# Load queues, builder engine and emission order changed in a fused state-space and local-attention kernel

## The chip, the cores and the metric

The kernel runs on one core of a Trainium2 chip. The metric is the device time of one execution in microseconds (us). A kernel's time is the median of several executions. The profile that is read here is one execution, recorded by the hardware profiler; its span runs from the first to the last instruction and is about 2 us shorter than the time (231.0 us of 232.73 for the kernel before).

The engines are named as in the profile: PE is the matrix engine (TensorE), PEld its weight loads, DVE is VectorE, ACT is ScalarE, POOL is GpSimd, SP is SyncE. A "q" behind a name (ACTq, SPq) means an instruction that issues a DMA transfer from that engine's queue.

## The reference, cut to what matters

Two independent parts share one output. Part A is a diagonal complex state-space layer over 2048 steps of width 448. Part B is attention of 16 heads, each query looking at 8 keys at distances 0, 2, ..., 14.

```python
# part A
dt = exp(log_dt);  Lam_bar = exp(dt * Lam)
B_bar = ((Lam_bar - 1.0) / Lam)[:, None] * Bmat
h_t = Lam_bar * h_{t-1} + B_bar @ x_t                  # 2048 steps
y = 2 * Re(C @ h) + x * Dskip
# part B
q, k, v = split(x @ wqkv);  W, dil = 8, 2
attn = softmax(q . k[pos - 2*w] * scale, masked at the start)
out_B = (attn @ v) @ wo
# concatenate(y, out_B)
```

Part A needs the powers of `Lam_bar` (1, 2, 3, 4, 8, ... 1024 and some negative ones). They come from four small parameter vectors (Lambda_re, Lambda_im, log_dt, Dskip, together under 4 KB) by a long chain of small VectorE operations, the "setup".

## The kernel before

The kernel cuts the recurrence into blocks, so that most of it becomes matmuls. Each complex power becomes a block matrix "identity pattern times coefficient": the ten power matrices `Mm`, four matrices `MB` for B, three matrices `MC` for C. Part B works in five groups: `proj` (projection to q, k, v), four `unit`s (scores, exponential, mask, values, normalisation), `wo` (output projection). The program uses a framework with a scheduler: the order of calls sets priorities, and the scheduler then orders each engine's instructions. Each engine works off its own list in order; several waits below come from that (one of 21.1 us on ScalarE).

The parts that the change touches (cuts marked `...`):

```python
    def loads_params(self):
        self.pr = pool.tile([NPR, P], bf16, name="pr")
        for i, src in enumerate((self.A_Lre, self.A_Lim, self.A_logdt, self.A_Dskip)):
            nc.scalar.dma_start(self.pr[NM * i:NM * (i + 1), 0:PL], src.rearrange("(m p) -> m p", p=PL))

    def loads_b(self):                     # B, 2 x 392 KB
        nc.gpsimd.dma_start(self.bX[0:PL], ...)
        nc.gpsimd.dma_start(self.bX[PL:P], ...)
    # loads_c: cn, 8 x 98 KB on nc.gpsimd;  loads2: wo_p, 4 x 98 KB on nc.gpsimd
    # load_x, loads_x: transposing loads of x on nc.sync;  wqkv: nc.scalar

    def setup(self):
        V.tensor_copy(self.pr[:, PL:P], self.pr[:, 0:PL])      # needs all four parameter loads
        nc.tensor.transpose(pp[:], self.pr[:], ident[0:NPR, 0:NPR])
        ...                                                    # some 60 small VectorE operations
        self.ScB = coeffs("ScB", sa, sb, 4)
        self.ScM = coeffs("ScM", pw_re[:, 3:13], pw_im[:, 3:13], NMAT)

    def build(self, eng, out, Sc, i):      # two inputs, both in SBUF
        eng.tensor_tensor(out, self.Dm[:]...to_broadcast([P, NM, 2, PL]),
                          Sc[:, i]...to_broadcast([P, NM, 2, PL]), op=ALU.mult)

    # main program
    b.loads()                              # x block, wqk
    ...
    a.loads_params()
    b.loads_v()
    b.prep()                               # VectorE permutes wqk into wqk_p
    b.load_x(0, 1)
    a.loads_b()
    ...                                    # first projection with a.setup() in it
    b.load_x(1, 0); b.load_x(1, 1)
    a.b_mats(V)
    a.loads_x()
    for hg in range(4):
        b.unit(0, hg)
    a.loads_c()
    for m in range(NM):
        a.b_variant(m)                     # bv_ps = bX x MB, evicted to Bv
    b.loads2()
    a.setup_dg()
    b.proj(1)
    a.mats(G)                              # ten power matrices on GpSimd
    for hg in range(4):
        b.unit(1, hg)
    b.wo(0)
    for hg in range(4):
        a.l1(hg)                           # l_ps: 112 matmuls with Bv
    b.proj(2)
    ...
    a.l2()                                 # e_ps: first use of the power matrices
```

The softmax here doesn't subtract the row's maximum and nothing guards it: scores larger than these inputs give would overflow.

Of the kernel before, what the change touches and what calls it, by code (L numbers as in the profile page):

```python
# [12 lines left out]
bf16 = mybir.dt.bfloat16  # L13
# [3 lines left out]
P = 128  # L17
KT = 4
H = 16
DH = 28  # L20
NM = 7
PL = 64
# [12 lines left out]
NMAT = len(MATS)  # L35
# [12 lines left out]
class PartB:  # L48
# [38 lines left out]
    def loads2(self):  # L87
        nc, pool = self.nc, self.pool
        self.wo_p = pool.tile([P, 4, D], bf16, name="wo_p")
        nc.gpsimd.memset(self.wo_p[:], 0.0)  # L90
        wo_v = self.B_wo.rearrange("(g h d) c -> h d g c", g=4, d=DH)
        for h in range(4):
            nc.gpsimd.dma_start(self.wo_p[32 * h:32 * h + DH, :, :], wo_v[h])

    def prep(self):
        nc, pool, V, G = self.nc, self.pool, self.nc.vector, self.nc.gpsimd
# [104 lines left out]
class PartA:  # L201
# [8 lines left out]
    def loads_params(self):  # L210
        nc, pool = self.nc, self.pool
        self.pr = pool.tile([NPR, P], bf16, name="pr")
        for i, src in enumerate((self.A_Lre, self.A_Lim, self.A_logdt, self.A_Dskip)):
            nc.scalar.dma_start(self.pr[NM * i:NM * (i + 1), 0:PL], src.rearrange("(m p) -> m p", p=PL))

    def loads_b(self):
        nc, pool = self.nc, self.pool
        self.bX = pool.tile([P, NM, D], bf16, name="bX", tag="r0")
        nc.gpsimd.dma_start(self.bX[0:PL], self.A_Bre.rearrange("(m p) d -> p m d", p=PL))
        nc.gpsimd.dma_start(self.bX[PL:P], self.A_Bim.rearrange("(m p) d -> p m d", p=PL))  # L220

    def loads_x(self):
        nc, pool = self.nc, self.pool
# [6 lines left out]
    def loads_c(self):  # L230
        nc, pool = self.nc, self.pool
        self.cn = pool.tile([112, 4, NM, 2, PL], bf16, name="cn", tag="c7")
        for ri, src in enumerate((self.A_Cre, self.A_Cim)):
            for a in range(4):
                nc.gpsimd.dma_start(self.cn[:, a, :, ri, :],
                                    src[112 * a:112 * (a + 1)].rearrange("p (m q) -> p m q", q=PL))

    def c_transpose(self):
# [10 lines left out]
    def setup(self):  # L249
        nc, pool, V, G = self.nc, self.pool, self.nc.vector, self.nc.gpsimd  # L250
# [51 lines left out]
        pw_re, pw_im = sh, ch  # L302
# [31 lines left out]
        V.tensor_tensor(self.Dm[:], ident[:, 0:PL], ident[:, PL:P], op=ALU.add)  # L334

        def coeffs(name, re, im, n, conj=False):
            Sc = pool.tile([P, n, NM, 2], bf16, name=name, tag=("ScM" if name == "ScM" else "ScB"))
            s0, s1 = (1.0, -1.0) if conj else (-1.0, 1.0)
            V.tensor_copy(Sc[0:PL, :, :, 0], re[0:PL])
            V.tensor_copy(Sc[PL:P, :, :, 1], re[PL:P])  # L340
            V.tensor_scalar(Sc[PL:P, :, :, 0], im[PL:P], s0, None, op0=ALU.mult)
            V.tensor_scalar(Sc[0:PL, :, :, 1], im[0:PL], s1, None, op0=ALU.mult)
            return Sc

        self.ScB = coeffs("ScB", sa, sb, 4)
        self.ScM = coeffs("ScM", pw_re[:, 3:13], pw_im[:, 3:13], NMAT)
        self.mkC = lambda: coeffs("ScC", pw_re[:, 0:3], pw_im[:, 0:3], 3, conj=True)
        self.dsk = dsk

# [15 lines left out]
                V.tensor_scalar(self.Dg[h, k, :], self.ident[h], self.dsk[h, m:m + 1], None, op0=ALU.mult)  # L365

    def mats(self, eng):
        self.M = self.pool.tile([P, NMAT, NM, 2, PL], bf16, name="Mm")
        for i in range(NMAT):
            self.build(eng, self.M[:, i], self.ScM, i)  # L370
# [131 lines left out]
@with_exitstack  # L502
def kernel(
    ctx: ExitStack,
    tc: tile.TileContext,
    A_x: bass.AP,
    A_Lambda_re: bass.AP,
    A_Lambda_im: bass.AP,
    A_B_re: bass.AP,
    A_B_im: bass.AP,  # L510
    A_C_re: bass.AP,
    A_C_im: bass.AP,
    A_log_dt: bass.AP,
    A_Dskip: bass.AP,
    B_x: bass.AP,
    B_wqkv: bass.AP,
    B_wo: bass.AP,
    out: bass.AP,
):
    nc = tc.nc  # L520
    pool = ctx.enter_context(tc.tile_pool(name="sb", bufs=1))
    psum = ctx.enter_context(tc.tile_pool(name="ps", bufs=1, space=bass.MemoryType.PSUM))
    ident = pool.tile([P, P], bf16, name="ident")
    nc.vector.memset(ident[:], 0.0)
    warm = pool.tile([1, 1], f32, name="warm")
    nc.vector.memset(warm[:], 0.0)
    nc.scalar.activation(warm[:], warm[:], ACT.Exp)

    class _Ps:
        def tile(self, shape, dtype, name, tag):  # L530
            return psum.tile(shape, dtype, name=name, tag=tag, bufs={"s": 2, "o": 1, "mm": 3}[tag])
    ps = _Ps()

    b = PartB(tc, B_x, B_wqkv, B_wo, out, pool, ps)
    a = PartA(tc, A_x, A_Lambda_re, A_Lambda_im, A_B_re, A_B_im, A_C_re, A_C_im, A_log_dt, A_Dskip,
              out, ident, pool, ps)
    V, G = nc.vector, nc.gpsimd
    b.loads()
    nc.gpsimd.affine_select(out=ident[:], in_=ident[:], compare_op=ALU.not_equal, fill=1.0, base=0,
                            pattern=[[-1, P]], channel_multiplier=1)  # L540
    b.mask = pool.tile([P, P], bf16, name="mask")
    nc.vector.memset(b.mask[:], 1.0)
    nc.gpsimd.affine_select(out=b.mask[:], in_=b.mask[:], compare_op=ALU.is_ge, fill=0.0, base=-1,
                            pattern=[[-1, P]], channel_multiplier=1)
    nc.gpsimd.affine_select(out=b.mask[:], in_=b.mask[:], compare_op=ALU.is_ge, fill=0.0, base=HALO,
                            pattern=[[1, P]], channel_multiplier=-1)
    a.loads_params()
    b.loads_v()
    b.prep()
    b.load_x(0, 1)  # L550
    a.loads_b()
    steps = b.proj_steps(0)
    for _ in range(PRE):
        next(steps)
    a.setup()
    for _ in steps:
        pass
    b.load_x(1, 0)
    b.load_x(1, 1)
    a.b_mats(V)  # L560
    a.loads_x()
    for hg in range(4):
        b.unit(0, hg)
    a.loads_c()
    for m in range(NM):
        a.b_variant(m)
    b.loads2()
    a.setup_dg()
    b.proj(1)
    a.mats(G)  # L570
    for hg in range(4):
        b.unit(1, hg)
    b.wo(0)
    for hg in range(4):
        a.l1(hg)
    b.proj(2)
    a.c_mats(V)
    a.c_transpose()
    for hg in range(4):
        b.unit(2, hg)  # L580
    b.wo(1)
    b.proj(3)
    a.l2()
    a.c_variants()
    for hg in range(4):
        b.unit(3, hg)
    b.wo(2)
    a.hfull(0)
    a.hfull(1)
    b.proj(4)  # L590
    b.unit(4, 0)
    a.hfull(2)
    a.hfull(3)
    b.unit(4, 1)
    a.hfull(4)
    a.hfull(5)
    b.wo(3)
    a.hfull(6)
    for s in range(4):
        if s >= 2:  # L600
            b.unit(4, s)
        for i in range(4):
            a.y(i, s)
    b.wo(4)
# [29 lines left out]
```

## Time and profile before

| | before |
|---|---|
| time, median of the runs beside the changed kernel's | 231.98 us (229.49 to 232.91) |
| span of the profiled run | 231.0 us |
| PE busy | 171.3 us, 74% |
| VectorE busy | 140.2 us, 61% |
| GpSimd busy | 35.3 us, 15% |

The page of the profile draws the span in 40 equal slices of 5.8 us. Each digit is the busy share of a slice in tenths; PEclk is the granted clock of PE in tenths of full speed; the DMA row is the mean busy share of the 16 DMA engines.

```profile
PE   0241197013445999999999999999989199999994
...
DVE  4200199999999793697441019909889964814261
...
PEclk9999999755575599999999999998579959999999
DMA  6999999600000000020000001100000200222212
```

PE is nearly idle in the first five slices (0 to 29 us), while the DMA engines are at work. VectorE is full from slice 5 to 12 (counted from 0), and PE is at most half busy from slice 7 to 12. Only from slice 13 (75 us) is PE mostly full. A change for the front part of the kernel can therefore win much, one for the back part little.

The timeline of the queue of ScalarE (start, duration, engine, line, instruction, times; in brackets idle time before it and what ended it) shows how the start is held up:

```profile
1.90 0.82 ACTq L214 DMA_DIRECT2D pr<-in_A_Lambda_re_dram  x1
...
4.93 0.30 ACTq L214 DMA_DIRECT2D pr<-in_A_Lambda_im_dram  x1
14.50 0.28 ACTq L214 DMA_DIRECT2D pr<-in_A_log_dt_dram  x1
22.43 0.27 ACTq L214 DMA_DIRECT2D pr<-in_A_Dskip_dram  x1
...
23.90 1.48 ACT L134 CAST qT<-qk_ps 128x480 bf16<-128x480 f32 x3 [21.14 <-DMA pr<-in_A_Dskip_dram]
```

The four tiny parameter loads are issued at 1.9, 4.9, 14.5 and 22.4 us. The compiled instruction list tells why: each but the first waits until an earlier load has landed:

```
before, ScalarE
5 L214 DMACopy pr<-in_A_Lambda_re_dram 7x64
6 L214 DMACopy pr<-in_A_Lambda_im_dram 7x64 [waits DMAHW0_49]
7 L214 DMACopy pr<-in_A_log_dt_dram 7x64 [waits DMAHW2_49]
8 L214 DMACopy pr<-in_A_Dskip_dram 7x64 [waits DMAHW4_49]
9 L76 DMACopy wv<-in_B_wqkv_dram 128x3x448 [waits DMAHW5_49]
```

In the program, DMAHW0 is the counter of the first load of weights, DMAHW2 that of the second load for the first x block, DMAHW4 that of the second load for the second x block. In the trace these three land at 4.91, 14.48 and 22.41 us, each 0.02 us before the issue that waits for it. So two of the four tiny loads wait for loads of x on SyncE's queue.

Behind these issues in ScalarE's list stand the first evictions of q, which come at 23.9 us after 21.1 us of idle time. On VectorE the copy that starts the setup waits for the last parameter:

```profile
7.02 1.47 DVE L98 COPY wqk_p<-wqk_nat 128x1792 bf16<-128x1792 bf16 x2 [3.15 <-DMA wqk_nat<-in_B_wqkv_dram]
27.90 0.17 DVE L256 COPY pr<-pr 28x64 bf16<-28x64 bf16 x1 [19.40 <-DMA pr<-in_A_Dskip_dram]
```

Then the second piece of trouble. GpSimd builds the ten power matrices from 37.9 us, as its timeline shows:

```profile
37.94 17.54 POOL L351 TENSOR_TENSOR Mm<-Dm,ScM 128x896 bf16<-128x896 bf16 x10 [16.77 <-DVE ScM L340]
```

These are VectorE's setup operations of the same time, and the four B matrices, from its timeline:

```profile
37.89 0.17 DVE L316 TENSOR_TENSOR sa<-lm_187,prT 128x7 f32<-128x7 f32 x1
38.09 1.56 DVE L318 TENSOR_TENSOR sa<-sa,t_190 128x7 f32<-128x7 f32 x1
39.68 1.61 DVE L319 TENSOR_TENSOR sa<-sa,rden 128x7 f32<-128x7 f32 x1
41.21 0.15 DVE L321 TENSOR_TENSOR t_190<-lm_187,prT 128x7 f32<-128x7 f32 x1
41.32 1.63 DVE L326 TENSOR_TENSOR sa<-kf,sa 128x21 f32<-128x21 f32 x1
...
53.97 2.37 DVE L341 TENSOR_SCALAR ScB<-sb 64x28 bf16<-64x28 f32 x1
...
57.01 4.08 DVE L351 TENSOR_TENSOR MB<-Dm,ScB 128x896 bf16<-128x896 bf16 x4
```

An operation on 7, 21 or 28 columns takes 0.15 to 0.18 us when it is not held up. The slow ones take 1.5 us and more, while a build lasts 1.79 us on average. The B matrices MB are complete at 61.1 us, and only then do the B variants (bv_ps), the second projection and the first layer (l_ps) follow. From 103.9 us on the first layer runs without a break:

```profile
103.88 19.72 PE L429 MATMUL l_ps<-xa,Bv 128*128 128x512 bf16 x88
```

### The profile page before, as it was taken

The page shows a single profiled execution, that of the slowest core. Times are in us where ns is not written, and L with a number is a line of the kernel's source. Part 1 is how long each engine was busy: PE and PEld are TensorE (multiplying, and loading weights), DVE is VectorE, ACT ScalarE, POOL GpSimd, SP SyncE. Part 2 cuts the span into 40 slices and gives each one's busy share as a digit, 9 for nine tenths or more (in the row PEclk, how much of TensorE's full clock was granted, in tenths as well). Part 3 has the DMA queues.
Part 4 walks back from the last instruction along what each step waited for, and adds up shares of the span by engine and source line. Part 5 has one row for each costly group of instructions (what it writes and reads, how often), then busy time and mean ns, then how long its engine had stood idle before and what let it go on. Part 6 is the DMA issues. An engine that isn't in the chain of part 4 may idle for free.

```text
span 231.0 us, 3482 instructions
## 1 busy us (share of the span) xinstructions
PE 171.3 (74%) x1348; PEld 86.9 (38%) x1348; DVE 140.2 (61%) x284; ACT 101.2 (44%) x177; POOL 35.3 (15%) x62
## 2 busy tenths in 40 slices
PE   0241197013445999999999999999989199999994
PEld 0010033002121244544444455465425096565652
DVE  4200199999999793697441019909889964814261
ACT  2000238113233566963335689665269148521311
POOL 8854004997000000000000000000000000000000
PEclk9999999755575599999999999998579959999999
DMA  6999999600000000020000001100000200222212
GB/s 195 155 157 161 207 213 189 147 0 3 0 0 0 1 3 0 19 59 0 0 3 0 0 1 38 38 0 0 3 0 19 60 0 3 70 79 76 67 61 70
DMA packets 26625, 12.11 MB, mean 52 GB/s; under 512 B 21056, under 2 KB 26048, under 8 KB 26608
## 3 DMA queue, kind: packets, MB, share of 16 engines
q1 hardware_dynamic: 24792, 8.67, 18.7%
q0 software_dynamic: 800, 2.01, 5.1%
q10 hardware_dynamic: 1016, 1.21, 1.7%
q8 instruction: 10, 0.16, 0.3%
q14 instruction: 7, 0.06, 0.1%
HBM read 3.21 MB, written 3.67 MB: 30 GB/s over the span
## 4 chain that ended last, share of the span: by engine, by line
PE 55%; DVE 25%; DMA 9%; ACT 5%; SPq 2%; issue 2%; ACTq 0%; DVEq 0%
PE l_ps L429 11%; PE qk_ps L129 11%; PE y_ps L488 9%; DMA xb_66<-in_B_x_dram 7%; PE v_ps L141 5%; PE bv_ps L394 4%; PE wo_ps L194 4%; DVE pt L169 4%; ACT pt L167 3%; PE cv_ps L411 2%; PE o_ps L175 2%; DMA pr<-in_A_Dskip_dram 2%; PE s_ps L160 2%; DVE tO L181 2%; DVE MB L351 2%
## 5 line engine op out<-in xcount | busy, mean ns | idle before, releaser
L167 ACT ACTIVATE pt<-s_ps 128x960 bf16<-128x960 f32 (+2 forms) x40 | 32.3, 878 | 21.1 <-PE s_ps L160 19.9
L169 DVE TENSOR_TENSOR pt<-pt,mask 128x960 bf16<-128x960 bf16 (+2 forms) x40 | 22.4, 560 | 29.8 <-ACT pt L167 29.6
L129 PE MATMUL qk_ps<-xb_66,wqk_p 128*128 128x480 bf16 (+5 forms) x96 | 22.7, 398 | 13.3 <-DMA xb_66<-in_B_x_dram 13.2
L129 PEld LDWEIGHTS <-wqk_p 128*128 128x128 bf16 x192 | 18.8, 118 | 29.4 <-issue 12.0
L429 PE MATMUL l_ps<-xa,Bv 128*128 128x512 bf16 x112 | 25.9, 379 | 0.0
L175 PE MATMUL o_ps<-pt,va 128*32 128x120 bf16 (+2 forms) x288 | 12.7, 230 | 17.6 <-DVE pt L169 14.5
L134 ACT CAST qT<-qk_ps 128x480 bf16<-128x480 f32 (+2 forms) x20 | 9.9, 507 | 27.5 <-DMA pr<-in_A_Dskip_dram 21.1
L351 POOL TENSOR_TENSOR Mm<-Dm,ScM 128x896 bf16<-128x896 bf16 x10 | 17.5, 1788 | 16.8 <-DVE ScM L340 16.8
L394 PE MATMUL bv_ps<-MB,bX 128*128 128x512 bf16 x28 | 13.1, 564 | 8.3 <-ACT Bv L399 3.8
L175 PEld LDWEIGHTS <-va 128*32 128x32 bf16 x288 | 7.1, 99 | 31.2 <-issue 28.1
L129 PE MATMUL qk_ps<-xb_67,wqk_p 128*128 128x480 bf16 (+5 forms) x96 | 18.6, 335 | 0.0
L194 PE MATMUL wo_ps<-wo_p,oT 128*120 128x448 bf16 (+2 forms) x72 | 17.5, 363 | 0.1
L160 PE MATMUL s_ps<-qT,kT 28*128 28x120 bf16 (+2 forms) x288 | 14.0, 226 | 3.3 <-ACT pt L167 3.1
L137 POOL MEMSET va<- 128x256 bf16 x5 | 1.6, 323 | 90.9 <-PE o_ps L175 90.9
L429 PEld LDWEIGHTS <-Bv 128*128 128x128 bf16 x112 | 10.6, 97 | 13.2 <-issue 1.4
L399 ACT CAST Bv<-bv_ps 128x512 bf16<-128x512 f32 x14 | 8.2, 586 | 15.8 <-PE bv_ps L394 15.6
L134 ACT CAST kT<-qk_ps 128x488 bf16<-128x488 f32 (+2 forms) x20 | 10.4, 518 | 7.1 <-PE qk_ps L129 7.0
L197 ACT CAST yb<-wo_ps 120x448 bf16<-120x448 f32 (+2 forms) x18 | 9.7, 579 | 8.3 <-PE wo_ps L194 8.3
L181 DVE STREAM_TRANSPOSE tO<-o_ps 128x480 f32<-128x480 f32 (+2 forms) x20 | 11.9, 597 | 1.6 <-PE o_ps L175 1.5
L256 DVE COPY pr<-pr 28x64 bf16<-28x64 bf16 x1 | 0.2, 169 | 19.4 <-DMA pr<-in_A_Dskip_dram 19.4
L186 DVE STREAM_TRANSPOSE oT<-on 128x480 bf16<-128x480 bf16 (+2 forms) x20 | 11.7, 586 | 0.2
L185 DVE TENSOR_TENSOR on<-tO,r 128x480 bf16<-128x480 f32 (+2 forms) x20 | 11.5, 576 | 0.2
(162 smaller groups left out, 270.7 us busy)
## 6 DMA issues: line engine op xcount, KB each, us to landing
out_dram<-ya SPq DMA_DIRECT2D x16, 112.0 KB, 1.7
out_dram<-yb SPq DMA_DIRECT2D x8, 105.0 KB, 1.9
out_dram<-yb SPq DMA_DIRECT2D x8, 98.0 KB, 1.8
wqk_nat<-in_B_wqkv_dram ACTq DMA_DIRECT2D x1, 672.0 KB
bX<-in_A_B_re_dram POOLq DMA_DIRECT2D x1, 392.0 KB, 10.1
bX<-in_A_B_im_dram POOLq DMA_DIRECT2D x1, 392.0 KB, 11.2
cn<-in_A_C_re_dram POOLq DMA_DIRECT2D x4, 98.0 KB, 12.4
cn<-in_A_C_im_dram POOLq DMA_DIRECT2D x4, 98.0 KB, 9.8
```

The source lines that it names most:

```text
L129: nc.tensor.matmul(ps[:, off:off + cnt], lhsT=self.wp[:, w, k, 4 * hg:4 * hg + 4].rearrange("p h d -> p (h d)"), rhs=self.xb[p][:, k, XP + ...
L134: nc.scalar.copy(dst[:, hg, 0:tot], ps[:, 0:tot])
L160: nc.tensor.matmul(sp[h // 2][:, h % 2, nq * i:nq * (i + 1)], lhsT=kT[32 * h:32 * h + DH, hg, koff[i]:koff[i] + P], rhs=qT[32 * h:32 * h + ...
L167: nc.scalar.activation(pt[:, :, 0:tot], sp[u][:, :, 0:tot], ACT.Exp, scale=scale)
L169: V.tensor_tensor(pv, pv, self.mask[:, 0:nq].unsqueeze(1).unsqueeze(1).to_broadcast([P, 2, nb, nq]), op=ALU.mult)
L175: nc.tensor.matmul(po[32 * h:32 * h + 32, nq * i:nq * (i + 1)], lhsT=va[:, i, 4 * hg + h, :], rhs=pts[h // 2][:, h % 2, nq * i:nq * (i + 1 ...
L181: V.transpose(tO[:, 0:nj].rearrange("p j d -> p (j d)"), po[:, 0:tot])
L194: nc.tensor.matmul(ps[0:nq, :], lhsT=oT[:, hg, nq * i:nq * (i + 1)], rhs=self.wo_p[:, hg, :], start=(hg == 0), stop=(hg == 3))
L351: eng.tensor_tensor(out, self.Dm[:].unsqueeze(1).unsqueeze(1).to_broadcast([P, NM, 2, PL]), Sc[:, i].unsqueeze(3).to_broadcast([P, NM, 2, ...
L394: nc.tensor.matmul(ps[:].rearrange("p s c -> p (s c)"), lhsT=self.bX[:, m, c0:c0 + P], rhs=self.MB[:, m].rearrange("p s h q -> p (s h q)") ...
L429: nc.tensor.matmul(ps[u][:], lhsT=self.Bv[:, s, KT * m + k, :], rhs=self.xT[:, k, s, :], start=(s == 0 and k == 0), stop=(k == KT - 1), sk ...
L488: nc.tensor.matmul(ps[:], lhsT=self.hl[m][:, s, i, :], rhs=self.Dv[s][:, m, :], start=(m == 0), stop=False, skip_group_check=True)
```

## The change

The intent: load what is needed first first, let VectorE instead of GpSimd build the power matrices, late enough not to delay anything, and give PE the second projection to do while VectorE works off setup and unit 0. There are four parts, called *parameters*, *bulk loads*, *matrices* and *order* below.

```diff
# parameters: first in the program, on GpSimd's queue
-            nc.scalar.dma_start(self.pr[NM * i:NM * (i + 1), 0:PL], ...)
+            nc.gpsimd.dma_start(self.pr[NM * i:NM * (i + 1), 0:PL], ...)
+    a.loads_params()
     b.loads()
 ...
-    a.loads_params()
     b.loads_v()
# bulk loads: bX, cn and wo_p from GpSimd's queue to SyncE's, bX ahead of the second x block
-        nc.gpsimd.dma_start(self.bX[...] / self.cn[...] / self.wo_p[...]
+        nc.sync.dma_start(self.bX[...] / self.cn[...] / self.wo_p[...]
     b.prep()
+    a.loads_b()
     b.load_x(0, 1)
-    a.loads_b()
# matrices: coefficients made on demand, matrices on VectorE behind the first layer
-            Sc = pool.tile([P, n, NM, 2], bf16, name=name, tag=("ScM" if name == "ScM" else "ScB"))
+            Sc = pool.tile([P, n, NM, 2], bf16, name=name, tag="ScB")
-        self.ScM = coeffs("ScM", pw_re[:, 3:13], pw_im[:, 3:13], NMAT)
+        self.mkM = lambda: coeffs("ScM", pw_re[:, 3:13], pw_im[:, 3:13], NMAT)
     def mats(self, eng):
+        self.ScM = self.mkM()
 ...
-    a.mats(G)
     for hg in range(4):
         b.unit(1, hg)
     b.wo(0)
     for hg in range(4):
         a.l1(hg)
+    a.mats(V)
     b.proj(2)
# order: second projection ahead of the B variants
     a.loads_c()
+    b.proj(1)
     for m in range(NM):
         a.b_variant(m)
     b.loads2()
     a.setup_dg()
-    b.proj(1)
```

More of the change, by code (lines that the diff above doesn't have):

```diff
@@ L92, in loads2 @@
         for h in range(4):
-            nc.gpsimd.dma_start(self.wo_p[32 * h:32 * h + DH, :, :], wo_v[h])
+            nc.sync.dma_start(self.wo_p[32 * h:32 * h + DH, :, :], wo_v[h])
     def prep(self):
@@ L213, in loads_params @@
         for i, src in enumerate((self.A_Lre, self.A_Lim, self.A_logdt, self.A_Dskip)):
-            nc.scalar.dma_start(self.pr[NM * i:NM * (i + 1), 0:PL], src.rearrange("(m p) -> m p", p=PL))
+            nc.gpsimd.dma_start(self.pr[NM * i:NM * (i + 1), 0:PL], src.rearrange("(m p) -> m p", p=PL))
     def loads_b(self):
@@ L218, in loads_b @@
         self.bX = pool.tile([P, NM, D], bf16, name="bX", tag="r0")
-        nc.gpsimd.dma_start(self.bX[0:PL], self.A_Bre.rearrange("(m p) d -> p m d", p=PL))
-        nc.gpsimd.dma_start(self.bX[PL:P], self.A_Bim.rearrange("(m p) d -> p m d", p=PL))
+        nc.sync.dma_start(self.bX[0:PL], self.A_Bre.rearrange("(m p) d -> p m d", p=PL))
+        nc.sync.dma_start(self.bX[PL:P], self.A_Bim.rearrange("(m p) d -> p m d", p=PL))
     def loads_x(self):
@@ L234, in loads_c @@
             for a in range(4):
-                nc.gpsimd.dma_start(self.cn[:, a, :, ri, :],
+                nc.sync.dma_start(self.cn[:, a, :, ri, :],
                                     src[112 * a:112 * (a + 1)].rearrange("p (m q) -> p m q", q=PL))
```

## The prediction

> **What bounds it now.** The span is 231.0 us and PE is busy 171.3 (74%). By stages: From 0 to 28 us PE has about 5 us of work: loads fill the DMA engines (0.6 to 1.27 of their time, 150 to 230 GB/s). From 28 to 100 us VectorE is the limit. From 100 us to the end PE is nearly full. The first-layer matmuls (l_ps) run without a break from 103.9 us; what is to win lies before.
>
> **Three waits there.**
> 1. Parameters. ScalarE issues the four small loads and each waits for an earlier transfer: issued at 1.9, 4.9, 14.5, 22.4 us. VectorE's setup starts only at 27.9 (19.4 us idle, released by the Dskip load), and ScalarE's first eviction of q waits 21.1 us behind the same issues.
> 2. GpSimd builds the power matrices from 37.9 to 55.4 us (10 x 1.79 us). Meanwhile eleven tiny VectorE operations take 1.53 to 1.66 us each, against 0.15 to 0.28 before: about 15 us. The Trainium skill ("SBUF — State Buffer", shared port pair) says a VectorE instruction with two SBUF inputs contends with a GpSimd one that reads SBUF and one fully blocks; the durations here, near GpSimd's 1.79, agree.
> 3. Unit 0, the B variants and the second projection run one after another (61 to 92 us).
>
> **What the change does.** Parameters go first on GpSimd and should land by 4 to 8 us. The bulk loads leave GpSimd; B follows the first x block on SyncE, so that block no longer shares with 2 MB of B, C and wo. I put its landing at 10 us instead of 14.5. ScalarE's queue is free for evictions after about 3 us. Twelve projection matmuls (0.42 us each) still precede the parameter transpose, so setup starts at about 15 us. Setup without slowed operations and without the ScM copies: about 11 us, MB 4 x 1.08: B matrices ready near 30 us instead of 61.  Then VectorE has unit 0 (12.4 us, the pace of later units), 14 Bv evictions (9.5), unit 1 (11.5): 33 us, perhaps 36 with waits, during which PE does projection 2 (9.4) and the variants. l_ps runs without a break at about 66 instead of 103.9: 38 us gained.
>
> **Given back.** Ten power matrices at 1.08 us plus ScM copies land on VectorE among the l_ps evictions; one step of l_ps lasts 1.8 us, an eviction 0.69 plus two matrices 2.85, so PE loses about 1 us in four or five steps: 4 us. The 127 us after are unchanged.
>
> **Prediction.** 232.7 - 38 + 4 = about 199 us; 191 to 209 should hold it 8 times in 10. Faster by over 2%: 0.96; within 2%: 0.03; slower: 0.01.
>
> **What the profile would show.** Right: first q eviction near 12 us, not 23.9; parameter copy before 9 us; setup operations all under 0.3 us; MB done near 30; uninterrupted l_ps near 66; small PE gaps in l_ps before VectorE evictions. Wrong: PE waiting for the second x block, B or wo on the single SyncE queue, whose issues wait for earlier transfers.
>
> **What would make me wrong.** The first x block landing as late as before: 4 to 5 us lost. Half granted clock, as from 42 to 83 us before: up to 5 us. In-order waits between VectorE, ScalarE and PE in the interleaved stage: up to 8 us. VectorE overloaded in l_ps: up to 6 us.

## The result

| | before | changed |
|---|---|---|
| time, median | 231.98 us (4 runs) | 192.94 us (192.16 to 193.89, 4 runs) |
| ratio of fast runs | | 0.8333, 95% interval 0.8248 to 0.8418 |
| span of the profiled run | 231.0 us | 191.9 us |
| PE busy | 171.3 us, 74% | 164.6 us, 86% |
| VectorE busy | 140.2 us, 61% | 133.5 us, 70% |
| GpSimd busy | 35.3 us, 15% | 8.9 us, 5% |
| mean granted PE clock | 0.889 | 0.956 |

A ratio is the mean time of one kernel's fast runs over that of the other's fast runs of the same rounds, so it is not quite the ratio of the medians. "Fast" is the state of the run; runs more than 1.5% above the fastest of the same kernel count as slow and are left out.

The time lies in the predicted range (191 to 209), 6 us under the predicted 199. The rows of PE, VectorE and the granted clock from the page of the changed kernel, with slices of 4.8 us now:

```profile
PE   0079994998999999999999999988945999999993
...
DVE  5027999799999999995029944988999278035161
...
PEclk9999998899999999999999999958995799999999
```

The idle front of PE is down to two slices, and PE is mostly full from there on. VectorE is just as full in the front part, but now PE works at the same time. The lines that answer to those of before, from the changed kernel's timeline of ScalarE:

```profile
12.48 0.56 ACT L134 CAST qT<-qk_ps 128x480 bf16<-128x480 f32 x1 [9.73 <-PE qk_ps L129]
```

From its timeline of VectorE:

```profile
9.80 0.17 DVE L256 COPY pr<-pr 28x64 bf16<-28x64 bf16 x1 [6.00 <-DMA pr<-in_A_Dskip_dram]
...
9.97 1.16 DVE L98 COPY wqk_p<-wqk_nat 128x1792 bf16<-128x1792 bf16 x2
...
24.64 0.18 DVE L326 TENSOR_TENSOR sa<-kf,sa 128x21 f32<-128x21 f32 x1
...
26.69 4.10 DVE L351 TENSOR_TENSOR MB<-Dm,ScB 128x896 bf16<-128x896 bf16 x4
```

And from its timeline of PE, the first layer from the point where it has PE to itself:

```profile
64.64 2.12 PE L430 MATMUL l_ps<-xa,Bv 128*128 128x512 bf16 x9
67.11 7.15 PE L430 MATMUL l_ps<-xa,Bv 128*128 128x512 bf16 x32 [0.35 <-DVE hl_899 L436]
74.71 8.00 PE L430 MATMUL l_ps<-xa,Bv 128*128 128x512 bf16 x36 [0.46 <-ACT hl_942 L434]
```

The first eviction of q comes at 12.48 us, the setup operations take 0.17 to 0.18 us, MB is complete at 30.8 us. Unit 1's last value matmuls start at 64.3 us, and from 64.6 us the first layer has PE to itself, as it had from 103.9 us before. The new brackets in the last two lines are small gaps of PE that the kernel before did not have.

One line was not foreseen. The parameter copy stands ahead of the permutation `wqk_p` in VectorE's list and waits until 9.80 us, because the parameters need 5.3 to 6.7 us from issue to landing. The first matmul therefore waits for `wqk_p`, not for the x block:

```profile
10.66 4.56 PE L129 MATMUL qk_ps<-xb_71,wqk_p 128*128 128x480 bf16 x12 [10.66 <-DVE wqk_p L98]
```

| landmark, us | before | predicted | changed |
|---|---|---|---|
| first q eviction | 23.9 | 12 | 12.5 |
| parameter copy | 27.9 | under 9 | 9.8 |
| setup starts (parameters transposed) | 28.4 | 15 | 15.4 |
| B matrices complete | 61.1 | 30 | 30.8 |
| first layer alone on PE | 103.9 | 66 | 64.6 |
| first power-matrix matmul (e_ps) | 154.2 | | 116.1 |
| end of span | 231.0 | | 191.9 |

So 39.2 us are gained by the time the first layer has PE to itself, 38.1 us are left at e_ps, and 39.1 us at the end. The gain is made in the front, as predicted. What the landmarks do not tell is which of the four parts made it.

### The profile page after: what moved, and what is told of

Its sections match the earlier page's. It is cut to its first block, busy times and chain, and to the rows that moved or that the text cites. A ratio compares the mean times of both kernels' runs of the same rounds, so it can differ in the third digit from the quotient of the medians.

```text
span 191.9 us, 3468 instructions
## 1 busy us (share of the span) xinstructions
PE 164.6 (86%) x1348; PEld 84.3 (44%) x1348; DVE 133.5 (70%) x294; ACT 99.8 (52%) x177; POOL 8.9 (5%) x42
## 4 chain that ended last, share of the span: by engine, by line
PE 66%; DVE 16%; ACT 9%; DMA 3%; issue 3%; POOL 1%; ACTq 0%; DVEq 0%; POOLq 0%
PE qk_ps L129 14%; PE l_ps L430 13%; PE y_ps L489 11%; PE v_ps L141 6%; PE wo_ps L194 5%; ACT pt L167 5%; PE o_ps L175 4%; DMA pr<-in_A_Dskip_dram 3%; PE s_ps L160 3%; PE cv_ps L412 3%; DVE pt L169 2%; PE bv_ps L395 2%; PE y_ps L493 2%; PE l_ps L462 2%; DVE MB L351 2%
## 5 line engine op out<-in xcount | busy, mean ns | idle before, releaser
L129 PE MATMUL qk_ps<-xb_71,wqk_p 128*128 128x480 bf16 (+5 forms) x96 | 21.9, 375 | 10.7 <-DVE wqk_p L98 10.7
L129 PEld LDWEIGHTS <-wqk_p 128*128 128x128 bf16 x192 | 17.4, 114 | 24.3 <-DVE wqk_p L98 10.7
L129 PE MATMUL qk_ps<-xb_72,wqk_p 128*128 128x480 bf16 (+5 forms) x96 | 18.5, 332 | 0.5 <-ACT hl_985 L434 0.5
L175 PE MATMUL o_ps<-pt,va 128*32 128x120 bf16 (+2 forms) x288 | 11.9, 221 | 5.9 <-DVE pt L169 4.0
L160 PE MATMUL s_ps<-qT,kT 28*128 28x120 bf16 (+2 forms) x288 | 15.8, 212 | 1.2 <-ACT pt L167 0.6
L194 PE MATMUL wo_ps<-wo_p,oT 128*120 128x448 bf16 (+2 forms) x72 | 16.6, 360 | 0.1
L160 PEld LDWEIGHTS <-kT 28*128 28x128 bf16 x288 | 8.4, 92 | 14.0 <-issue 12.0
L144 ACT CAST va<-v_ps 128x448 bf16<-128x448 f32 x18 | 9.6, 532 | 5.3 <-PE v_ps L141 5.3
L499 DVE CAST ya<-y_ps 128x448 bf16<-128x448 f32 x8 | 5.0, 620 | 10.1 <-PE y_ps L493 10.1
L185 DVE TENSOR_TENSOR on<-tO,r 128x480 bf16<-128x480 f32 (+2 forms) x20 | 11.5, 574 | 0.2
L351 DVE TENSOR_TENSOR Mm<-Dm,ScM 128x896 bf16<-128x896 bf16 x10 | 10.4, 1074 | 0.0
L194 PEld LDWEIGHTS <-oT 128*120 128x120 bf16 (+2 forms) x72 | 8.6, 130 | 3.8
```

The source lines that it names most:

```text
L129: nc.tensor.matmul(ps[:, off:off + cnt], lhsT=self.wp[:, w, k, 4 * hg:4 * hg + 4].rearrange("p h d -> p (h d)"), rhs=self.xb[p][:, k, XP + ...
L160: nc.tensor.matmul(sp[h // 2][:, h % 2, nq * i:nq * (i + 1)], lhsT=kT[32 * h:32 * h + DH, hg, koff[i]:koff[i] + P], rhs=qT[32 * h:32 * h + ...
L175: nc.tensor.matmul(po[32 * h:32 * h + 32, nq * i:nq * (i + 1)], lhsT=va[:, i, 4 * hg + h, :], rhs=pts[h // 2][:, h % 2, nq * i:nq * (i + 1 ...
L194: nc.tensor.matmul(ps[0:nq, :], lhsT=oT[:, hg, nq * i:nq * (i + 1)], rhs=self.wo_p[:, hg, :], start=(hg == 0), stop=(hg == 3))
L351: eng.tensor_tensor(out, self.Dm[:].unsqueeze(1).unsqueeze(1).to_broadcast([P, NM, 2, PL]), Sc[:, i].unsqueeze(3).to_broadcast([P, NM, 2, ...
```

## The experiments

Theory at this point, from the prediction: there are three separate waits. The parameters part removes the first, the matrices part the second, the order part the third, and the bulk loads part lets the x block land earlier. Rivals: the bulk loads are what held up the whole start; VectorE's slow operations have a cause other than GpSimd; the stage is bound by VectorE whatever order PE has. The first four runs change one thing in the kernel before, the next four undo one part of the changed kernel, and the last four follow up. The order part alone, on the kernel before, was not run. All kernels gave correct results except the two that are wrong on purpose. Each of these three groups of four ran on another chip (`b_memset2`, shown under 3, is one of the last four), so the ratio to the kernel before, measured in the same rounds, is the fairer comparison between groups; differences of medians across groups are rough.

| run | median us | ratio to before, 95% interval |
|---|---|---|
| parameters alone | 219.52 | 0.948 (0.940 to 0.955) |
| matrices alone | 219.73 | 0.950 (0.942 to 0.958) |
| bulk loads alone | 216.42 | 0.932 (0.924 to 0.941) |
| changed kernel | 192.94 | 0.833 (0.825 to 0.842) |
| all but parameters | 190.78 | 0.822 (0.815 to 0.829) |
| all but bulk loads | 194.91 | 0.842 (0.836 to 0.848) |
| all but matrices | 206.62 | 0.892 (0.887 to 0.897) |
| all but order | 208.22 | 0.899 (0.893 to 0.906) |
| all but parameters and bulk loads | 205.96 | 0.889 (0.881 to 0.898) |

### 1. Parameters alone (`b_params`)

```diff
-            nc.scalar.dma_start(self.pr[...
+            nc.gpsimd.dma_start(self.pr[...
# and the call moved to the front, as in the change
```

> The kernel before with one part alone: the four parameter loads first on GpSimd. My theory (the start waits for the parameters): first eviction of q before 16 us instead of 23.9, setup starts near 19 us instead of 28.3 (the x block still lands at 14.5), the slowed VectorE operations stay, so about 10 us less: 222 us. Rival (the start is bound by the mass of bulk loads, the parameters only travel with it): parameters land no earlier than about 20 us, under 4 us gained: 228 us or more.

Measured: 219.52 us, 11.5 less than before. The first eviction no longer waits and the setup starts at 15 us, earlier than the 19 that I expected, because the x block also came in time:

```profile
10.36 4.44 PE L129 MATMUL qk_ps<-xb,wqk_p 128*128 128x480 bf16 x12 [10.36 <-DVE wqk_p L98]
```

These twelve matmuls run without a break, whereas in the kernel before the fourth waited for the x block until 14.5 us. GpSimd now issues the parameters ahead of its first bulk load, which moves that load from 2.5 to 5.3 us; that the x block profits from just this was not tested by itself. The setup operations stay slow (up to 1.66 us), as expected, and MB is complete only at 51.7 us. The theory holds for the time; the x block landed earlier than the theory had it.

### 2. Matrices alone (`b_mats`)

The diff is the *matrices* part above, on the kernel before.

> The kernel before with one part alone: power matrices on VectorE after the first-layer evictions in program order. My theory (GpSimd's builds slow VectorE's setup): the eleven operations of 1.5 to 1.7 us fall under 0.3 us, B matrices ready near 46 us instead of 61, about 13 us less: 219 us. Rival (those operations are slow because of the transposes landing then or of their own dependencies): they stay slow and the ten builds add up to 10 us: 232 to 242 us.

Measured: 219.73 us, 11.3 less. The setup operations fall to 0.18 us although they have the same dependencies and follow the same loads and transposes, so neither was the cause. MB is complete at 44.9 us. The rival falls.

```profile
38.01 0.18 DVE L327 TENSOR_TENSOR tb<-ch,sb 128x21 f32<-128x21 f32 x1
...
40.78 4.08 DVE L351 TENSOR_TENSOR MB<-Dm,ScB 128x896 bf16<-128x896 bf16 x4
```

### 3. GpSimd busy without reading (`b_memset`, `b_memset2`, wrong results on purpose)

```diff
# b_memset
         for i in range(NMAT):
-            self.build(eng, self.M[:, i], self.ScM, i)
+            eng.memset(self.M[:, i], 0.0)
+            eng.memset(self.M[:, i], 0.0)
# b_memset2: first a one-column copy that waits for the coefficients
+            eng.tensor_copy(self.M[:, i, 0, 0, 0:1], self.ScM[:, i, 0, 0:1])
```

> Wrong result on purpose. The kernel before, but GpSimd fills the power matrices with twenty memsets instead of ten two-input products: busy about as long (near 18 us) in the same stretch, but reading nothing from SBUF. Theory that reads through the shared port block VectorE: VectorE's setup operations of 1.5 to 1.7 us fall under 0.3 us and about 14 us are gained: 218 us. Rival that any GpSimd work, or the transposes landing at that time, slows them: they stay above 0.8 us and the time stays near 231 us.

Measured: 225.62 us (its profiled run was slow), and a failed experiment. The memsets wait for nothing, so they ran from 23.2 to 39.0 us, ahead of the setup. There they hit something else:

```profile
30.41 8.59 DVE L256 COPY pr<-pr 28x64 bf16<-28x64 bf16 x1 [19.17 <-DMA pr<-in_A_Dskip_dram]
```

The parameter copy, 0.17 us long in the lines of the other runs shown here, took 8.59 us and ended at 39.0, when the memsets had ended. With GpSimd idle again the setup operations took 0.18 us. So writes alone can hold up a VectorE copy from SBUF to SBUF, and for much longer than one of the memsets, which take 0.86 us each. What reads do to two-input operations was left open.

> Wrong result on purpose. The kernel before, with GpSimd's ten products replaced by ten one-column copies that wait for the coefficients and then twenty memsets, so that GpSimd is busy without reading, about 16 us, in the stretch where setup was slow. Theory that reads block reads: VectorE's two-input setup products take under 0.3 us there; its one-input copies and scalings may still be held up. Rival that any GpSimd work in SBUF slows them all: the products stay above 0.8 us.

Measured: 216.44 us in a single run, whose state is unknown. The memsets started late this time, at 47.7 us, because the list of GpSimd has another instruction ahead of them that waits for a load. The setup ran with GpSimd idle but for the ten one-column copies (37.5 to 38.8 us) and was fast, which agrees with run 2. The memsets then ran beside unit 0, whose mask and normalisation products also have two inputs in SBUF:

```profile
47.70 1.63 POOL L371 MEMSET Mm<- 128x896 bf16 x2
```

VectorE's timeline in the same run:

```profile
50.31 0.59 DVE L169 TENSOR_TENSOR pt<-pt,mask 128x960 bf16<-128x960 bf16 x1
50.83 0.64 DVE L185 TENSOR_TENSOR on<-tO,r 128x480 bf16<-128x480 f32 x1
```

They took 0.59 to 0.66 us, as the same operations do in unit 0 of run 2 with GpSimd idle (0.59 to 0.66 us). The Trainium skill ("SBUF — State Buffer", section "Who interferes with whom") says that a VectorE instruction with two SBUF inputs contends with a GpSimd instruction that reads SBUF, not with one that only writes it. These lines agree. The counterpart is in run 1, where the same mask product ran beside the builds, which do read:

```profile
27.08 2.17 DVE L169 TENSOR_TENSOR pt<-pt,mask 128x960 bf16<-128x960 bf16 x1
```

Two of the five mask products there took 2.17 and 2.14 us; the other three, each right behind an operation that had been held up, took 0.64 or 0.65. So one and the same product is held up beside builds and not beside memsets. Three limits remain. Each side is one profiled run, a memset differs from a build in more than its reads, and the setup products themselves never ran beside memsets. For them the step from "GpSimd's builds" to "the builds' reads" stays an inference. And two inputs are not the whole condition: two of the ten slow setup operations have one (1.57 and 2.37 us), as had the copy of the parameters.

### 4. Bulk loads alone (`b_bulk`)

The diff is the *bulk loads* part, on the kernel before.

> The kernel before with one part alone: the B, C and output-projection loads on SyncE in the new order. My theory: the x block lands near 10 us instead of 14.5, but the parameters still wait on ScalarE's queue for earlier transfers, so setup does not start before 18 us; between 0 and 8 us less: 224 to 232 us. Rival (the bulk loads on GpSimd are what held everything back): most of the 39 us comes from this part: under 212 us.

Measured: 216.42 us, 14.6 less, where I had expected 0 to 8. It is the largest of the three single gains that were measured, though far from the rival's "most of the 39". The parameters, still on ScalarE behind the weights, no longer hang back: they are issued at 1.9, 2.7, 5.2 and 7.6 us, the copy is at 12.3 us, and the first matmul at 8.4 us. So the first of my three waits goes with this part too.

```profile
7.64 0.28 ACTq L214 DMA_DIRECT2D pr<-in_A_Dskip_dram  x1
```

And from VectorE's timeline in the same run:

```profile
12.26 0.17 DVE L256 COPY pr<-pr 28x64 bf16<-28x64 bf16 x1 [3.41 <-DMA pr<-in_A_Dskip_dram]
```

### 5. All but parameters (`u_params`)

The four lines of the *parameters* part reversed in the changed kernel.

> The changed kernel with one part undone: parameter loads back on ScalarE behind the weights. My theory: they wait for earlier transfers again, setup starts 5 to 12 us later and the gain shrinks by 4 to 10 us: 197 to 203 us. Rival (with the bulk loads moved, ScalarE's loads are as quick): within 2 us of 193.

Measured: 190.78 us. The theory falls and the rival holds, and more: the kernel without this part has the lowest median of all. Its fast runs (190.3 to 191.7) lie below those of the changed kernel (192.2 to 193.9), but they come from different chips, and the two intervals of the ratio to the kernel before overlap (0.815 to 0.829 and 0.825 to 0.842), so in time the 2 us are not shown clear of noise.

The timeline of ScalarE's queue in this run, its last parameter issue:

```profile
7.55 0.28 ACTq L214 DMA_DIRECT2D pr<-in_A_Dskip_dram  x1
```

Then its timeline of PE:

```profile
8.08 4.68 PE L129 MATMUL qk_ps<-xb,wqk_p 128*128 128x480 bf16 x12 [8.08 <-DMA pr<-in_A_Dskip_dram]
```

And of VectorE:

```profile
12.15 0.17 DVE L256 COPY pr<-pr 28x64 bf16<-28x64 bf16 x1 [3.59 <-DMA pr<-in_A_Dskip_dram]
```

The compiled list shows the larger part of the reason: with the B loads on SyncE ahead of the second x block, the counters fall differently. Lambda_im has none to wait for, log_dt waits for the first load of weights, and Dskip for the first load of x (counter DMAHW1) instead of the fourth. The other part is that this load lands sooner, at 7.53 us instead of 9.58 in the kernel before. That is 2 us; in the kernel before Dskip's own wait ended at 22.41.

```
all but parameters, ScalarE
5 L214 DMACopy pr<-in_A_Lambda_re_dram 7x64
6 L214 DMACopy pr<-in_A_Lambda_im_dram 7x64
7 L214 DMACopy pr<-in_A_log_dt_dram 7x64 [waits DMAHW0_49]
8 L214 DMACopy pr<-in_A_Dskip_dram 7x64 [waits DMAHW1_49]
9 L76 DMACopy wv<-in_B_wqkv_dram 128x3x448 [waits DMAHW2_49]
```

The parameters land later than in the changed kernel (copy at 12.15 instead of 9.80 us), but just before PE has finished the twelve matmuls that stand ahead of their transpose. And here the permutation of the weights is not behind them in VectorE's list, so the first matmul starts at 8.08 instead of 10.66 us. (The bracket of that matmul names the Dskip load, but such releasers are inferred from events: the matmul does not read the parameters. What it reads are the x block and the permuted weights, and the permutation ran in two pieces from 7.40 to about 8.6 us.) The 2.5 us persist: the long stretch of the first layer that begins at 67.11 us in the changed kernel begins at 64.61 us here.

```profile
64.61 7.15 PE L430 MATMUL l_ps<-xa,Bv 128*128 128x512 bf16 x32 [0.35 <-DVE hl L436]
```

### 6. All but matrices (`u_mats`)

```diff
# the matrices part reversed, then
+    a.mats(G)          # again behind b.proj(1) and a.setup_dg(), ahead of unit 1
```

> The changed kernel with one part undone: power matrices on GpSimd as early as their inputs allow. My theory: VectorE's setup operations are 1.5 us and more again while GpSimd builds, B matrices ready near 45 us instead of 31; PE has the second projection to do meanwhile, so 8 to 14 us more: 201 to 207 us. Rival (VectorE is relieved of ten builds of 1.07 us): faster by 1 to 3 us.

Measured: 206.62 us, 13.7 more than the changed kernel by the medians. GpSimd builds from 24.9 to 41.5 us, and ten setup operations between 25.1 and 41.5 us take 1.5 us and more again. MB is complete at 46.2 us instead of 30.8. From the timelines of GpSimd and then of VectorE:

```profile
24.92 16.53 POOL L351 TENSOR_TENSOR Mm<-Dm,ScM 128x896 bf16<-128x896 bf16 x10 [16.35 <-DVE ScM L340]
```

```profile
28.30 1.63 DVE L326 TENSOR_TENSOR sa<-kf,sa 128x21 f32<-128x21 f32 x1
```

That VectorE is relieved of ten builds does not show.

### 7. All but order (`u_order`)

The *order* part reversed in the changed kernel.

> The changed kernel with one part undone: second projection emitted behind the B variants. My theory: PE idles while VectorE works off setup and unit 0, then VectorE idles during the projection; 5 to 10 us more: 198 to 203 us. Rival (the stage is bound by VectorE whatever PE's order): within 2 us of 193.

Measured: 208.22 us, 15.3 more, more than the 5 to 10 that I expected. The table of stretches (window; span; busy us of PE, PEld, DVE, ACT, POOL with instruction counts; granted clock; DMA share; GB/s), for the changed kernel and then for this one:

```profile
25.00:35.00 10.00, 7.07 (x59) 2.90 (x58) 9.34 (x22) 5.97 (x10) 0.00 (x0) 0.84 1.00 149
35.00:45.00 10.00, 9.50 (x109) 4.22 (x109) 9.06 (x20) 6.85 (x12) 0.45 (x2) 0.99 0.99 156
```

```profile
25.00:35.00 10.00, 4.82 (x50) 2.13 (x50) 9.01 (x21) 4.60 (x7) 0.00 (x0) 0.57 1.05 155
35.00:45.00 10.00, 4.67 (x66) 2.09 (x63) 9.79 (x20) 3.40 (x5) 0.00 (x0) 0.50 0.90 166
```

VectorE is as busy in both. PE has little to do until VectorE lets it go on, and it also runs at about half clock (0.50 to 0.57) there, so that the B variants take longer. In the changed kernel the projection fills the same stretch, and the clock stays up (0.84 to 0.99). The Trainium skill ("TensorE: Matmul & The Clock Gate", "What's actually happening") says that the clock is throttled by default and released by sustained activity; these lines agree, but no run here changed the clock alone. A caution: the scheduler also moved the ten power matrices, to 57.2 to 67.3 us, in the shadow of the projection, so this run does not undo the order and nothing else.

### 8. All but bulk loads (`u_bulk`)

The *bulk loads* part reversed in the changed kernel.

> The changed kernel with one part undone: B, C and output-projection loads back on GpSimd. My theory: first matmuls wait for the x block until about 14.5 us instead of 10.7, everything after shifts by it: 3 to 5 us more, 196 to 198 us. Rival (the transposes are slow by themselves, contention does not matter): within 1 us of 193.

Measured: 194.91 us, 2.0 more by the medians, less than expected and for another reason. The intervals of the ratio overlap (0.836 to 0.848 and 0.825 to 0.842), so this too is not shown clear of noise. The first twelve matmuls start at 10.23 us and do not wait for the x block. The load of the v weights comes late instead (the v projection stands still for 2.14 us at 20 us), and VectorE loses about 2 us to memsets on GpSimd. PE's timeline:

```profile
22.21 2.62 PE L141 MATMUL v_ps<-wv,xb 128*128 128x448 bf16 x13 [2.14 <-DMA wv<-in_B_wqkv_dram]
```

MB is complete only at 37.4 us in this run, 6.6 us later than in the changed kernel, and the time is just 2.0 us longer. With the second projection ahead of them, the B variants do not wait for MB: in the changed kernel the first of them starts at 42.3 us, 11.5 after MB is complete.

### 9. All but parameters and bulk loads (`b_mats_order`)

The *matrices* and *order* parts on the kernel before.

> The changed kernel with two parts undone, parameters and bulk loads both as before. Undone one at a time they cost -2 and +2 us. Theory that they are two cures of one wait (the parameters held up on ScalarE's queue by transfers that the bulk loads slow): undone together, setup starts at about 28 us again and the time is 10 to 15 us above the changed kernel: 203 to 208 us. Rival (neither matters once the matrices and the order are changed): under 196 us.

Measured: 205.96 us in the median of four runs; the two fast ones are 203.3 and 204.9. Undone one at a time the two parts cost -2 and +2 us by the medians, neither clear of noise, undone together some 11 (the fast runs' mean of 204.1 less 193.0). The profiled run, a slow one, has the parameters issued at 1.9, 5.0, 15.3 and 23.4 us again and the setup starting at 28.9. So they are two cures of one wait, and one of them is enough. Which transfer a parameter load waits for is set by the counters, as run 5 showed; that the bulk loads slow that transfer, as I had put it, is the smaller part.

### 10. Copy of the parameters on ScalarE (`a_actcopy`)

```diff
-        V.tensor_copy(self.pr[:, PL:P], self.pr[:, 0:PL])
+        nc.scalar.copy(self.pr[:, PL:P], self.pr[:, 0:PL])
```

> The changed kernel, but the copy that doubles the parameters runs on ScalarE instead of ahead of the weight permutation in VectorE's queue. Theory that this copy's wait for the parameters (until 9.8 us) delays the first matmul from about 8.2 to 10.7 us and everything after it: 2 to 2.5 us less, 190.5 us. Rival (the first x block lands no earlier than 10 us): the same as the changed kernel, 193 us.

Measured: 191.28 us, ratio 0.835 (0.829 to 0.841). The trace does what the theory says, to a smaller amount: the first matmul at 9.07 instead of 10.66 us (the weights landed at 8.0, and their permutation took 1.56 us), and the long stretch of the first layer at 65.84 instead of 67.11.

```profile
9.07 4.98 PE L129 MATMUL qk_ps<-xb,wqk_p 128*128 128x480 bf16 x12 [9.07 <-DVE wqk_p L98]
```

The gain of 1.3 us in the trace fits the medians, but the ratio to the kernel before is not better than the changed kernel's, because on this chip the fast runs of the kernel before were faster as well (228.7 to 230.2). In time the gain is not shown clear of noise.

### 11. Power matrices on GpSimd at the late place (`a_both`)

```diff
# with the copy on ScalarE, and
-    a.mats(V)
+    a.mats(G)
```

> As the run with the copy on ScalarE, and the power matrices on GpSimd at their late place, behind the first-layer matmuls in program order, where VectorE mostly evicts from PSUM. Theory: the PE gaps in the first layer (about 1.5 us before evictions that waited behind VectorE's builds) go, and GpSimd slows few VectorE operations: 188.5 to 190 us. Rival (GpSimd's reads hold up unit 1's two-input operations and the three C matrices there): no gain or up to 2 us lost against 190.5.

Measured: 202.18 us, about 11 more than run 10: a miss, and not in the way that the rival said. GpSimd builds from 64.5 to 81.3 us, and VectorE's evictions of the first layer run beside it undisturbed (0.65 to 0.69 us each), while one product with two inputs in SBUF takes 0.90 us instead of 0.61. But then VectorE stands still:

```profile
71.69 0.69 DVE L436 CAST hl<-l_ps 128x512 bf16<-128x512 f32 x1 [1.11 <-PE l_ps L430]
81.36 0.18 DVE L339 CAST ScC<-kf 64x21 bf16<-64x21 f32 x1 [8.98 <-POOL Mm L351]
```

PE's timeline in the same run:

```profile
65.63 9.13 PE L430 MATMUL l_ps<-xa,Bv 128*128 128x512 bf16 x40 [0.35 <-DVE hl L436]
83.78 10.43 PE L430 MATMUL l_ps<-xa,Bv 128*128 128x512 bf16 x36 [9.03 <-DVE hl L436]
```

ScC, the coefficients of the C matrices, waits 9 us for the last build. The diff has the reason: the change put the coefficients ScM and ScC under one tag, and here they share one buffer, which is free only when all ten builds have read it. VectorE executes in order, so the evictions behind ScC wait too, PE runs out of PSUM buffers and stands still for 9 us, and then its matmuls take 0.29 us each instead of 0.23 (36 in 10.4 us, 40 in 9.1 before), with a granted clock of 0.77 from 83 to 95 us against 1.00 from 60 to 75. With the builds on VectorE the shared buffer costs nothing, as ScC follows them in the same list anyway. A version with a buffer of its own for ScM was not run; whether late building on GpSimd pays stays open.

## Why the prediction was right

**The sum.** Predicted: 232.7 - 38 + 4, about 199. Measured: 192.94. The 6 us between are the term "given back" (predicted 4 us; the gain is 39.2 us when the first layer has PE to itself and still 39.1 at the end, so about nothing in the net: 1.1 us are lost by e_ps and 1.0 come back after it, and what brought them back was not looked into), the first layer 1.4 us earlier than predicted, and 0.7 us by which the median of the kernel before came out lower with a fourth run.

**What bounds the kernel.** Right: all was gained ahead of the uninterrupted first layer, and the 127 us after it stayed 127 us (231.0 - 103.9 and 191.9 - 64.6).

**Wait 1, the parameters.** The wait was real, worth about 11 us, and is gone. "Parameters go first on GpSimd" was given as its cure. (The text on record says "should land by 4 to 8 us".) The runs show that the bulk loads part alone removes it as well, that with it the parameters part is not needed, and that it then delays PE's first matmul by 2.6 us in the traces (about 2 us by the medians, not clear of noise), because the landing at 9.7 us instead of 4 to 8 holds up the permutation of the weights behind it in VectorE's list. The attribution to one part is the step that failed, and it failed because the counters of ScalarE's loads move when other loads change their queue. The two gains are not additive.

**The x block.** Predicted at 10 us once B, C and wo leave GpSimd. The number was right: its second load, issued at 2.2 us, took 7.8 to land, so 10.0. But PE's start at 10.66 us, near the predicted 10, was set by the permutation of the weights behind the parameter copy, which the prediction did not have; that the landmarks of q and of the setup fit to 0.5 us is in part luck. And in `b_params` and `u_bulk` it was in time too, with the bulk loads still on GpSimd behind the parameters. It did not need the move to SyncE.

**Wait 2, the slow setup.** Right: 0.17 us instead of 1.5 and more without GpSimd beside it (`b_mats`), slow again with it (`u_mats`), 11 us gained alone and 14 lost when undone. Slips: the slow operations were ten, one for each build, not eleven, one of them took 2.37 us, outside the stated 1.53 to 1.66, and two have only one input, so the cited rule on two inputs does not cover them.

**Wait 3, one stage after the other.** Right in kind. Its undoing costs 15 us, more than the 9.4 us of the projection, with PE's clock at about half in that stretch. That run also moved the power matrices, so the 15 us are not the order's alone.

**Given back in the first layer.** The size was off, and the mechanism is shown only in part. "PE loses about 1 us in four or five steps: 4 us" was to be read in PE gaps before evictions; there are four, of 0.35, 0.46, 0.46 and 0.27 us, 1.5 us in all. The first, the only one that the profile puts down to a VectorE eviction, lies ahead of the first build (67.12 us) and is there in run 11 too, where GpSimd builds; so at most 1.2 us belong to the builds. At the other three the profile names ScalarE's eviction, but a VectorE eviction held up behind two builds ends within 0.04 us of it. VectorE did need 2.6 us for one eviction and two matrices where a step of PE lasts 1.8, but ScalarE takes more than half of the evictions, and three PSUM buffers probably take up much of the rest; that was not tested.

**What would have made it wrong** did not come: the x block was not late, SyncE's single queue held up nothing (the last of wo is issued at 39.4 us), and in the stage from 30 to 60 us VectorE was busy 28.0 us of the 30 and the granted clock was 0.94.

## What to carry to other kernels

When an engine issues loads and also computes, look for what its issues wait for: four loads of 0.9 KB held this kernel for about 11 us, and either taking them off that queue or moving other loads, which changed what they waited for, was enough. In an in-order list, a short operation that waits for a late input delays everything behind it, as the parameter copy did with 2 us and the shared coefficient buffer with 9. Test the parts of a bundled change one by one, adding and undoing: here two parts cured the same wait, and the bundle without one of them was at least as fast.

## What the Trainium skill lacked or had wrong

- "SBUF — State Buffer" ("SBUF: two separate sides", "Who interferes with whom"): the shared port pair is described as held for one instruction, by whichever of the two starts first. Here a 0.17 us VectorE copy waited 8.59 us while GpSimd ran memsets of 0.86 us one after the other, and ended only with the last of them. The pages that I read do not say that a chain of GpSimd instructions can keep the port from VectorE.
- "DMA: Bandwidth & Descriptors" ("Anatomy of one DMA — SWDGE (gpsimd) path"): fits the time as about 2.0 us plus bytes over 436 GB/s. Four loads of 0.9 KB issued from GpSimd took 5.3 to 6.7 us from issue to landing while other queues were loading at 170 to 240 GB/s. A figure for a small load from issue to landing while other queues are busy is lacking.
- No page that I read has the rotation of completion counters (a matter of the compiled program) that made a 0.9 KB load wait for a load of x on another queue: log_dt and Dskip issued at 14.5 and 22.4 us in the kernel before, at 4.9 and 7.5 us when the counters fell differently.
